# A state-space and MLP block on one core: layer norm in chunks, the middle loop in another order, the fifth scan block in pieces under the output stage

## Chip, cores and metric

One core of a Trainium2 chip. The metric is device time in microseconds (us) of the whole kernel; medians of several runs are quoted. TensorE is called PE, its weight loads PEld, VectorE DVE, ScalarE ACT, the engine that issues transfers SP. Matmuls write into a memory of their own, PSUM. The granted clock is the share of PE's full speed that the profile shows. One execution of the kernel before was slower (485.2 us, mean granted clock 0.82). A line number such as L450 is a line of the kernel that is being spoken of; the kernel before and the changed one have different numbers for the same work.

## The reference

Two branches work on the layer-normed input `xn` (2048 tokens, 640 channels, bf16) and are added to `x`. Branch A is a complex diagonal recurrence over time, branch B a shifted MLP with a second layer norm.

```python
def A(x, ...):                       # 640 complex states
    Bu = einsum("bld,pd->blp", x, B_bar)
    for t in range(L): h = Lam_bar * h + Bu[:, t]
    return 2 * einsum("blp,dp->bld", hseq, C).real + x * Dskip
def B(x, w1, w2, w3, w4):
    h = gelu(layernorm(x) @ w1)
    # ... four channel groups shifted by +1, -1, +2, -2 tokens ...
    x1 = x + shifted(h) @ w2
    return x1 + gelu(layernorm(x1) @ w3) @ w4      # 640 -> 1536 -> 640
xn = layernorm(x)
return x + A(xn, ...) + B(xn, ...)
```

## The kernel before

The 640 states are five blocks of 128 partitions, the 2048 tokens four groups of 512. Each block is projected (`bur`, `bui`), rotated by tables of sine and cosine so that the complex recurrence becomes two real ones, scanned over all 2048 tokens, and rotated back into `hTr`, `hTi`. Gelu is written as x times sigmoid. Names that the profiles use: `x1n` is the input of the third matmul (w3) after its layer norm, `psh` that matmul's result in PSUM, `sg` its sigmoid, `h3h` the product of the two, `acc` the sum that the w4 matmuls build from it; `xrxi` holds a block's projection (later its scan), `bp` a part of its rotation, `ctab` and `stab` its tables; `psy` is the result of the output matmuls. The parts that matter, cut with `...`:

```python
# head: layer norm over all 2048 tokens at once
with tc.tile_pool(name="lrow", bufs=1) as lrow, ..., tc.tile_pool(name="lnp", bufs=1, PSUM) as lnp:
    ...
    for tg in range(TG):
        ...                                        # s1_ps, s2_ps: sums by ones-matmuls
        nc.scalar.copy(out=S1row[:, cols], in_=s1_ps[:])
        nc.scalar.copy(out=S2row[:, cols], in_=s2_ps[:])
    nc.vector.tensor_scalar_mul(out=mean[:], in0=S1row[:], scalar1=inv_d)
    ...                                            # var, Ln, Exp, c1, second Ln and Exp, all 128x2048 f32
    for j in range(DB): ...                        # xnT = xT*r1b + c1b
    for j in range(DB): ...                        # skip: xT += dskip*xnT
# w1 stage
for tg in range(TG): ...                           # xnn, 25 matmuls, sigmoid, copy, h1T pieces

def a_block(b, btr, bti):
    ...                                            # projections, sine tables, rotation
    nc.vector.tensor_tensor_scan(out=gr, data0=rho_bc, data1=bpr, initial=0.0, ...)   # 2048 columns
    nc.vector.tensor_tensor_scan(out=gi, data0=rho_bc, data1=bpi, initial=0.0, ...)
    ...                                            # rotation back

def phase3_h3_half(x1n, fh):
    for f in range(FH):                            # 6 of 12
        ...                                        # psh: 5 matmuls
        nc.scalar.activation(out=sg3[:], in_=psh[:], func=ACT.Sigmoid, scale=GELU_SIG_A)
        nc.vector.tensor_tensor(out=h3h[:, f, :], in0=sg3[:], in1=psh[:], op=ALU.mult)

run_a(0)
st = phase3_tg_pre(0)                              # w2, layer norm 2 -> x1n
h3a = phase3_h3_half(x1n_cur, 0)
phase3_w4_half(st, h3a, 0)
for r in range(TG):
    run_a(r + 1)                                   # whole block r+1
    h3b = phase3_h3_half(x1n_cur, 1)
    if r + 1 < TG: st_next = phase3_tg_pre(r + 1) ...
    phase3_w4_half(st, h3b, 1)
    if r + 1 < TG:
        ...
        h3a = phase3_h3_half(x1n_cur, 0)
        phase3_w4_half(st, h3a, 0)
# output stage: C transposed and scaled, 200 matmuls into psy, fob = xT + psy, 80 transposes, copies, store
```

## Time and profile before

| | before |
|---|---|
| median of 6 runs (range) | 478.42 us (477.19 to 485.2) |
| span of the profiled run | 483.3 us |
| mean granted PE clock in it | 0.82 |
| busy PE / DVE / ACT | 305.0 / 295.7 / 223.4 us |

The profiled run of the kernel before was the slow one of the six (485.2 us), so that some us of what follows are its state and not the kernel. The next view cuts its span at marks of the program: first sigmoid 78.4, first w2 matmul 118.1, rotation of blocks 1 to 4 at 178.5, 248.2, 317.0 and 387.5, dense output matmuls from 429.4. Columns: start and end, length, busy us (and count of instructions) of PE, PEld, DVE, ACT and GpSimd, granted clock, share of the DMA engines, GB/s.

```profile
0.00:78.40 78.40, 18.09 (x50) 6.00 (x51) 39.17 (x80) 31.69 (x26) 2.49 (x7) 0.74 0.36 90
78.40:118.10 39.70, 34.02 (x131) 13.61 (x130) 26.72 (x55) 29.68 (x52) 0.00 (x0) 0.85 0.08 17
...
248.20:317.00 68.80, 48.43 (x201) 20.51 (x200) 45.60 (x54) 34.00 (x43) 0.00 (x0) 0.84 0.13 34
...
429.40:483.30 53.90, 48.02 (x256) 21.52 (x256) 14.50 (x21) 18.22 (x80) 0.00 (x0) 0.94 0.14 49
```

Compare PE's busy time with the length: in the head PE is busy 18 of 78 us, in a round of the middle 48 of 69, in the last stage 48 of 54. Only the last stage is near a limit of one engine.

### The profile page before, as it was taken

To read this page: it belongs to the slowest core of one execution; us is meant where nothing else is said; L and a number is where in the kernel's file an instruction comes from. 1 tells how busy PE (TensorE), PEld (TensorE's weight loads), DVE (VectorE), ACT (ScalarE), POOL (GpSimd) and SP (SyncE) were. 2 spreads that over 40 slices of the span, in tenths; PEclk is the share of its full clock that TensorE was granted. 3 is DMA by queue.
4 is the path that set the end of the run, shared out by engine and by line. 5 is a ranking of instruction groups with operands and counts; after the bars stand their busy time and mean duration, and the time that the engine had idled before them with its cause. 6 is when DMAs were issued, how large, how long until landed. Compare 5 with 4: busy or idle time off the path is not lost.

```text
span 483.3 us, 3602 instructions
## 1 busy us (share of the span) xinstructions
PE 305.0 (63%) x1260; PEld 125.9 (26%) x1260; DVE 295.7 (61%) x400; ACT 223.4 (46%) x334; POOL 2.5 (1%) x7
## 2 busy tenths in 40 slices
PE   2270007798504996285985558982849980679995
PEld 0020002233201342032432123430314430224442
DVE  0203999953999469958149867079635099762221
ACT  5338404769641963495142694241892230213332
POOL 2000000000000000000000000000000000000000
PEclk9996555989855999596998687997687997889998
DMA  9830010011100111110202010201010200431111
GB/s 179 207 130 1 0 37 31 15 26 22 23 0 1 54 33 34 31 41 0 83 11 57 0 42 1 81 1 41 0 41 4 79 14 0 97 40 54 56 54 56
DMA packets 38753, 20.23 MB, mean 42 GB/s; under 512 B 28624, under 2 KB 38096, under 8 KB 38736
## 3 DMA queue, kind: packets, MB, share of 16 engines
q1 hardware_dynamic: 38736, 20.01, 16.1%
q8 instruction: 10, 0.16, 0.1%
q14 instruction: 7, 0.06, 0.0%
HBM read 11.47 MB, written 2.62 MB: 29 GB/s over the span
## 4 chain that ended last, share of the span: by engine, by line
PE 42%; DVE 36%; ACT 10%; SPq 6%; DMA 4%; issue 2%; ACTq 0%; DVEq 0%
PE acc L469 6%; PE ps L393 6%; PE psh L450 6%; DVE xrxi L374 5%; DVE xrxi L377 4%; PE psy L537 4%; PE bur L337 4%; PE psy L542 4%; PE ps L269 3%; PE bui L343 3%; DVE h3h L456 3%; SPq L93 2%; PE pt L551 1%; DMA li_b<-in_A_Lambda_im_dram 1%; DVE bp L365 1%
## 5 line engine op out<-in xcount | busy, mean ns | idle before, releaser
L450 PE MATMUL psh<-x1n,w_sb 128*128 128x512 bf16 x240 | 65.4, 423 | 52.7 <-DVE x1n L428 46.2
L469 PE MATMUL acc<-h3h,w4f 128*128 128x512 bf16 x240 | 60.2, 399 | 11.9 <-DVE h3h L456 11.9
L455 ACT ACTIVATE sg<-psh 128x512 bf16<-128x512 f32 x48 | 28.4, 597 | 75.4 <-PE psh L450 43.9
L269 PE MATMUL ps<-xnn,w_sb 128*128 128x512 bf16 x100 | 29.3, 451 | 41.4 <-DMA w_sb<-in_B_w_dram 39.0
L393 PE MATMUL ps<-h1T,w_sb 128*128 128x512 bf16 x100 | 29.4, 463 | 35.2 <-DVE h3h L456 34.4
L450 PEld LDWEIGHTS <-w_sb 128*128 128x128 bf16 x240 | 25.1, 105 | 90.7 <-issue 66.3
L456 DVE TENSOR_TENSOR h3h<-sg,psh 128x512 bf16<-128x512 bf16 x48 | 32.4, 683 | 17.8 <-ACT sg L455 17.8
L537 PE MATMUL psy<-hTr,CTr 128*128 128x512 bf16 x100 | 38.2, 394 | 5.8 <-DVE CTr L522 4.1
L542 PE MATMUL psy<-hTi,CTi 128*128 128x512 bf16 x100 | 38.5, 397 | 0.6 <-DVE CTi L526 0.4
L552 ACT COPY rowbuf<-pt 128x128 bf16<-128x128 bf16 x80 | 18.2, 267 | 42.7 <-PE pt L551 16.0
L469 PEld LDWEIGHTS <-w4f 128*128 128x128 bf16 x240 | 24.4, 102 | 43.4 <-issue 14.9
L548 DVE TENSOR_TENSOR fob<-xT,psy 128x512 bf16<-128x512 bf16 x20 | 13.7, 687 | 33.7 <-PE psy L542 33.2
L365 DVE TENSOR_TENSOR bp<-xrxi,ctab 128x2048 bf16<-128x2048 bf16 x5 | 6.1, 1223 | 42.6 <-ACT xrxi L341 42.6
L337 PE MATMUL bur<-xnT,btr 128*128 128x512 bf16 x100 | 26.7, 392 | 3.2 <-DMA btr<-in_A_B_re_dram 3.2
L269 PEld LDWEIGHTS <-w_sb 128*128 128x128 bf16 x100 | 11.2, 112 | 58.8 <-issue 50.8
L343 PE MATMUL bui<-xnT,bti 128*128 128x512 bf16 x100 | 25.8, 391 | 0.0
L393 PEld LDWEIGHTS <-w_sb 128*128 128x128 bf16 x100 | 11.5, 115 | 52.9 <-issue 44.8
L341 ACT CAST xrxi<-bur 128x512 bf16<-128x512 f32 x20 | 11.8, 590 | 28.0 <-PE bur L337 28.0
L357 ACT ACTIVATE stab<-u_r 128x2048 bf16<-128x2048 f32 x5 | 9.6, 1910 | 30.7 <-DVE hTi L383 30.2
L374 DVE TENSOR_TENSOR_SCAN xrxi<-rho_col,bp 128x2048 bf16<-128x2048 f32 x5 | 22.1, 4415 | 0.0
L377 DVE TENSOR_TENSOR_SCAN xrxi<-rho_col,bp 128x2048 bf16<-128x2048 f32 x5 | 22.0, 4397 | 0.0
L178 PE MATMUL s_ps<-xT,ones_bf 128*128 128x512 bf16 x20 | 9.0, 484 | 20.4 <-DMA xT<-in_A_x_dram 11.3
(133 smaller groups left out, 480.9 us busy)
## 6 DMA issues: line engine op xcount, KB each, us to landing
w4f<-in_B_w_dram SPq DMA_DIRECT2D x48, 160.0 KB, 2.2
out_dram<-rowbuf SPq DMA_DIRECT2D x4, 640.0 KB, 3.2
w_sb<-in_B_w_dram SPq DMA_DIRECT2D x1, 1920.0 KB, 8.0
w_sb<-in_B_w_dram SPq DMA_DIRECT2D x2, 800.0 KB, 5.8
btr<-in_A_B_re_dram SPq DMA_TRANSPOSE x25, 2.3
bti<-in_A_B_im_dram SPq DMA_TRANSPOSE x25, 2.3
xT<-in_A_x_dram SPq DMA_TRANSPOSE x5, 5.1
CTr<-in_A_C_re_dram SPq DMA_TRANSPOSE x5, 2.9
```

Source lines behind the costliest of these rows:

```text
L269: nc.tensor.matmul(ps[:], lhsT=w1_sb[:, j, i * P : (i + 1) * P], rhs=xnn[:, j, :], start=(j == 0), stop=(j == DB - 1),)
L337: nc.tensor.matmul(bur[:], lhsT=btr[:, j, :], rhs=xnT[:, j, cols], start=(j == 0), stop=(j == DB - 1),)
L343: nc.tensor.matmul(bui[:], lhsT=bti[:, j, :], rhs=xnT[:, j, cols], start=(j == 0), stop=(j == DB - 1),)
L374: nc.vector.tensor_tensor_scan(out=gr, data0=rho_bc, data1=bpr, initial=0.0, op0=ALU.mult, op1=ALU.add,)
L377: nc.vector.tensor_tensor_scan(out=gi, data0=rho_bc, data1=bpi, initial=0.0, op0=ALU.mult, op1=ALU.add,)
L393: nc.tensor.matmul(ps[:], lhsT=w2_sb[:, j, i * P : (i + 1) * P], rhs=h1T[:, j, 2 + tg * 512 : 2 + tg * 512 + 512], start=(j == 0), stop=(j ...
L450: nc.tensor.matmul(psh[:], lhsT=w3_sb[:, j, ff * P : (ff + 1) * P], rhs=x1n[:, j, :], start=(j == 0), stop=(j == DB - 1),)
L455: nc.scalar.activation(out=sg3[:], in_=psh[:], func=ACT.Sigmoid, scale=GELU_SIG_A)
L456: nc.vector.tensor_tensor(out=h3h[:, f, :], in0=sg3[:], in1=psh[:], op=ALU.mult)
L469: nc.tensor.matmul(accs[i][:], lhsT=w4fs[ff][:, i * P : (i + 1) * P], rhs=h3h[:, f, :], start=False, stop=(ff == FB - 1),)
L537: nc.tensor.matmul(psy[:], lhsT=CTr[:, b, i * P : (i + 1) * P], rhs=hTr[:, b, cols], start=(k == 0), stop=False,)
L542: nc.tensor.matmul(psy[:], lhsT=CTi[:, b, i * P : (i + 1) * P], rhs=hTi[:, b, cols], start=False, stop=(b == NPB - 1),)
```

## The change

Its intent is to stop the engines from taking turns. Five things are changed:

1. The first layer norm runs in four chunks of 512 tokens, straight from PSUM; its Ln and Exp share one table, loaded early.
2. The memory is laid out anew: the layer norm no longer takes over the memory of the parameter tiles, its PSUM sums have two buffers each, and the projection of block 0 goes into the w1 stage. The skip products come after the w1 work of their group.
3. `h3x`: ScalarE copies `psh` to bf16, so that VectorE's product reads no PSUM.
4. The middle loop pairs block r with token group r and spreads the parts of the block between the halves of the MLP.
5. The fifth block is scanned in four pieces inside the output stage.

```diff
-        for j in range(DB): ...                     # full-width layer norm, then all of skip
+        for tg in range(TG):
+            r2b, last_exp = ln1_tg(tg)              # 512 columns, load_ln_exp(...) early
+            r2bs.append(r2b)
+        for tg in range(TG):
+            with tc.issue_after(last_exp.ins):
+                ph2_tg(tg, r2bs[tg])                # w1 stage
+                a_bu_tg(bt0, tg)                    # projection of block 0
+            skip_tg(tg)
 ...
                 nc.scalar.activation(out=sg3[:], in_=psh[:], func=ACT.Sigmoid, scale=GELU_SIG_A)
-                nc.vector.tensor_tensor(out=h3h[:, f, :], in0=sg3[:], in1=psh[:], op=ALU.mult)
+                h3x = bsq.tile([P, 512], BF16, name="h3x")
+                nc.scalar.copy(out=h3x[:], in_=psh[:])
+                nc.vector.tensor_tensor(out=h3h[:, f, :], in0=sg3[:], in1=h3x[:], op=ALU.mult)
 ...
+        st_cur = b1_pre(0)
+        a_tables(0)
         for r in range(TG):
-            run_a(r + 1) ...
+            h3a = b2_h3_half(st_cur, 0)
+            a_fwd(b)                                # b = r; rotation
+            b3_w4_half(st_cur, h3a, 0, accs)
+            a_scans(b)
+            if r + 1 < TG: st_next = b1_pre(r + 1)
+            h3b = b2_h3_half(st_cur, 1)
+            a_back(b)
+            if b + 1 < NPB:
+                a1(b + 1)                           # projection of the next block
+                a_tables(b + 1)
+            b3_w4_half(st_cur, h3b, 1, accs)
 ...
         for tg in range(TG):
+            a_last(NPB - 1, [tg])                   # fifth block, 512 columns
             ...                                     # output matmuls of tg
```

## The prediction

> **What bounds the kernel now.** I read the busy table first, to see whether one engine is near its limit.
>
> ```profile
> PE 305.0 (63%) x1260; PEld 125.9 (26%) x1260; DVE 295.7 (61%) x400; ACT 223.4 (46%) x334; POOL 2.5 (1%) x7
> ```
>
> None is. TensorE and VectorE are busy 63% and 61%; together that is 601 us in a span of 483, so for at least three quarters of the span not both are working: they largely take turns. The waits of the whole span say who hands the turn to whom (microseconds in total, times, longest):
>
> ```profile
> PE psh L450 <- DVE x1n L428: 46.2, 4, 24.5
> DVE bp L365 <- ACT xrxi L341: 42.6, 4, 13.9
> PE ps L269 <- DMA w_sb<-in_B_w_dram: 39.0, 1, 39.0
> PE ps L393 <- DVE h3h L456: 34.4, 3, 11.5
> ```
>
> Three of these are one loop: PE waits for VectorE's normalised rows (L428), then VectorE waits until PE and ScalarE have delivered the next block's projection (L341), then PE waits for the h3h products that stand in VectorE's queue behind the scans (L456). The fourth is the head: PE has nothing to do until the layer norm over all 2048 tokens and its weights are there. Next the chain that ended last, one round of the middle (start, length, what):
>
> ```profile
> 248.18 1.23 DVE bp L365
> ...
> 256.87 4.33 DVE xrxi L374
> 261.21 4.32 DVE xrxi L377
> ...
> 271.83 7.15 PE ps L393 x25
> ...
> 288.02 1.28 ACT L417
> 291.04 0.76 DVE x1n L427 x2
> 292.19 5.00 PE psh L450 x15
> 297.19 1.13 PE acc L463 x5
> 298.32 3.37 PE psh L450 x15
> 301.69 6.74 PE acc L469 x30
> 308.43 1.13 PE bur L337 x5
> ...
> 316.96 1.22 DVE bp L365
> ```
>
> The chain alternates: VectorE 24.6 us (rotate, two scans, rotate back), PE and ScalarE 19.4 us (L393, statistics, tables of sine, Ln, Exp) up to x1n, then PE 25 us (psh 9.5, acc 6.7, the projections 8.5). The round is 316.96 - 248.18 = 68.8 us. The stretches of that size confirm that no engine fills it (stretch, length, then busy by engine):
>
> ```profile
> 239.70:308.40 68.70, 48.33 (x201) 20.47 (x200) 45.59 (x53) 34.00 (x43) 0.00 (x0) 0.84 0.13 34
> ```
>
> PE 48 and DVE 46 of 68.7 (an overlap-free sum would be 94): there are some 20 us of alternation to win per round, and a floor near 48.
>
> **What the Trainium skill says.** "TensorE: Matmul & The Clock Gate", Part 1 (the HAM clock gate): a PE idle for about 3.4 us falls to half rate and needs about as long to recover. The trace agrees: after the 7.4 us idle at 292.19 fifteen matmuls take 5.0 us, a later fifteen 3.4 us. Each long idle so costs 1.5 us beyond itself. "ScalarE: Activation LUTs", What ACT_TABLE_LOAD costs: 1283 ns and a drain of about 1380 ns. Here the load is 1.28 us and the next activation starts 0.02 us later (288.02+1.28, Exp at 289.32), so I take 1.3 per switch. "VectorE: DVE Perf Modes", Mode 1× and Mode 2×_1P: operands in PSUM run at the base rate, packed bf16 in SBUF at twice that. The trace agrees: h3h, with one PSUM operand, averages 683 ns, x1n from bf16 in SBUF 416 ns; back to back 0.60 and 0.34.
>
> **The change part by part.** I followed the compiled order of each engine in the changed kernel and put on it the start-to-start times of this trace (matmul of 512 columns 0.225, bf16 pass over 2048 columns 1.14, over 512 0.34, sigmoid plus copy pair 0.97, table load 1.3).
>
> *Head.* The layer norm goes from one pass over 2048 tokens to four of 512. Before, a chain of full-width f32 passes runs from 35.8 (mean) to 68 and the first sigmoid starts at 78.4. After, the VectorE parameter arithmetic, now with 4.6 us of table argument among it, ends near 29; then mean, and chunks 0 and 1 give xnT by 29+1+4+5.2+5.2 = 45. ScalarE has the tables of block 0 (four passes of 1.9) and about nine table loads in the same queue and sits at the end: its last Exp at 61, one load, first sigmoid at **62.5**. VectorE has chunks 2 and 3 done then as well (63). Gain 16.
>
> *w1 stage with the projections of block 0.* Per 512 tokens VectorE has xnn 5 x 0.34, nine h1T pieces 3.3, skip 5 x 0.55: 7.7; PE has 35 matmuls, 7.9; ScalarE 5 pairs and 2 copies, 5.9. Four groups plus 4.6 us of table argument, less what ran already: 33 us, to **96**. Before, this point (first L393) was 118. Gain 22 so far; the DMA wait is inside it.
>
> *First round.* Block 0's rotation starts at 96.5. In VectorE's queue stand rotation 6.8, x1 3.0, statistics 1.8, scan 4.3, x1n and x 5.1, scan 4.3, h3h 2.0, rotation back 6.8: 34.5. The rest of the round as below, 30: next rotation at **161**; before, block 1's was at 178.5. Gain 17.5 so far. (The old order started block 1's rotation before block 0's tokens had finished their second h3 half; the new one doesn't, so 4.5 us of the 22 are given back.)
>
> *Steady rounds.* Between x1n and the projections the old chain had psh half, identity and acc half: 308.43-292.19 = 16.2, and x1n 2.3 before it (289.98 to 292.19). The new order puts the half-0 matmuls after the projections, where they run under the next block's rotation and first scan (11 us of VectorE work against 15 matmul groups, 30 acc later); only half 1 remains in between, at the pace of ScalarE: six sigmoid-and-copy pairs, 5.8. So 68.8 - 16.2 - 2.3 + 5.8 = 56.1. The h3x copy is 12 x 0.48 = 5.8 us more ScalarE and 12 x 0.26 = 3.1 us less VectorE per round; only half 1 of it is on the path and is in the 5.8. Walking the queues for the other hops gives 54; I use **55.5**, twice: 216.5, 272. Before these were 69.7 and 68.8 (248.2, 317). Gain 27.
>
> *Fifth block.* Its rotation and scans leave the middle and go, in four pieces, under the output matmuls, where VectorE was busy 17.8 of 57.3 us. So one round vanishes: before, block 4's rotation started at 387.5 and dense output matmuls at 429.4. After, block 3's at 272: rotation, scans and back with half-0 matmuls 22-24, half-1 pairs behind a table load to 31, projections with sine passes between the copies to 43, acc to 47, C transposes (ten at 1.27 us, once the w3 buffer is free) to 46 and their VectorE scaling to 48.5, first piece of the fifth block (12 x 0.34 + 2 x 1.1) to 54, with 24 of 200 output matmuls (5.4 us) done meanwhile. Then 429.4 to 483.3 = 54 less 5.4: 272 + 54 + 48.6 = 374.6. From block 3's rotation to the end it was 483.3 - 317 = 166.3 and becomes 102.6: gain 64, on top of the 45 already won at that point.
>
> Sum: 96.5 + 64.5 + 111 + 102.6 = **375** of span. The profiled run was a slow one (485.2 against the median 478.4), which would take 4 off; run times exceed the span by 2; hand-offs between engines that I left out (0.1 to 0.2 us each, some 30 on the path) add about 5. Prediction **378**.
>
> **Rivals.** (a) *ScalarE becomes the link.* h3x copies, sigmoid, squares, sine passes, Ln and Exp share one in-order queue, with five table loads per round. For: in the compiled order the squares of x1 stand between sine passes, and a sigmoid pair with its own table load between them and Ln. Its sum is about 37 us per round, so it isn't a throughput bound, but it can delay x1n or the projections. 60 to 62 per round: 392. (b) *VectorE is the bound.* About 41 us per round in an in-order queue; h3h products stand before x1n in it, as they stood behind the scans before. If each such place costs 2 us: 385 to 390. Against: the cheaper h3h and the lost PSUM read. (c) *Less alternation than I think, and full-rate PE.* With 45 us of matmuls per round and no 11 us idles, PE stays warm; 50 per round and a head at 55: 358. (d) *The head gives nothing*, because many short passes pay their fixed cost and the loads of Ln/Exp repeat: 16 us lost, 392. (e) *No gain at all* would need the rounds to stay at 69; even then the removed fifth round saves over 30 us.
>
> **Range and chances.** Errors of 3 us per round in four rounds, 8 in the head and 5 in the end, partly independent, give about -18/+24: 360 to 402. All rivals are faster than before by over 10%, so 0.97 for faster; what is left is for a stall that I did not see in the order.
>
> **What would show it.** Rotation starts in the changed profile at about 96, 161, 216 and 272; the first sigmoid near 62; the wait of psh for x1n falls from 46 to under 15 us in total, that of L393 for h3h from 34 to under 8; h3h products near 416 ns; the full-width scans number four pairs; output matmuls dense for the last 50 us. VectorE's busy sum drops to about 280, ScalarE's rises to about 248 (48 h3x copies of 0.59). I am wrong if rounds exceed 62 (then see who ends the projections' wait), if the first sigmoid comes after 72, or if output matmuls wait for the fifth block's pieces.

## The result

| | before | after |
|---|---|---|
| median (range, runs) | 478.49 us (476.9 to 485.2, 16) | 377.74 us (375.85 to 379.41, 8) |
| span of the profiled run | 483.3 us (slow) | 376.9 us (fast) |
| busy PE / DVE / ACT | 305.0 / 295.7 / 223.4 us | 291.4 / 286.8 / 239.5 us |

The ratio is 0.789 (95% interval 0.7875 to 0.7909). A ratio here is the mean time of one kernel's runs over that of the other's of the same rounds, so it isn't quite the ratio of the medians quoted. Executions over 1.5% slower than the fastest of the same kernel are left out of the means. The time is 100.7 us less by the medians, and the prediction of 378.0 holds.

The busy table of the changed kernel:

```profile
PE 291.4 (77%) x1260; PEld 122.4 (32%) x1260; DVE 286.8 (76%) x509; ACT 239.5 (64%) x401; POOL 2.5 (1%) x7
```

The same number of matmuls, and nearly the same VectorE work, in a span shorter by a fifth: the time came from waits and not from work. Here are the waits of the whole span that answer to the four shown before:

```profile
ACT sg L482 <- DVE h3h L485: 24.0, 11, 3.6
...
PE psh L477 <- ACT h3x L484: 14.5, 9, 2.8
...
PE psh L477 <- DVE x1n L462: 8.7, 1, 8.7
DVE bp L263 <- ACT xrxi L228: 8.4, 3, 3.6
...
PE acc L500 <- DVE h3h L485: 2.7, 1, 2.7
```

`psh` waits for `x1n` 8.7 us instead of 46.2, and once instead of four times; the rotation waits for the projections 8.4 us instead of 42.6; the 34.4 us of w2 matmuls behind `h3h` are gone. What is new is short and frequent: `psh` and the sigmoid wait for a buffer (14.5 and 24.0 us). Now the stretches, cut at the same marks, with the rotation of blocks 0 to 3 at 96.8, 160.0, 212.9 and 266.8:

```profile
0.00:62.00 62.00, 23.82 (x55) 7.02 (x56) 40.12 (x123) 42.89 (x56) 2.49 (x7) 0.76 0.38 80
62.00:96.50 34.50, 29.68 (x126) 12.59 (x126) 33.48 (x86) 24.20 (x47) 0.00 (x0) 0.94 0.19 65
96.50:160.00 63.50, 49.77 (x215) 20.97 (x214) 51.82 (x76) 44.52 (x61) 0.00 (x0) 0.92 0.13 36
160.00:212.90 52.90, 45.84 (x197) 19.57 (x195) 42.12 (x52) 37.73 (x54) 0.00 (x0) 0.94 0.15 41
212.90:266.80 53.90, 47.15 (x212) 20.43 (x210) 41.67 (x52) 38.98 (x55) 0.00 (x0) 1.00 0.18 49
266.80:319.00 52.20, 45.39 (x200) 19.68 (x199) 45.72 (x63) 32.95 (x50) 0.00 (x0) 0.97 0.29 64
319.00:376.90 57.90, 49.78 (x263) 22.13 (x262) 31.84 (x60) 18.22 (x80) 0.00 (x0) 0.94 0.13 46
```

Against the table before: the head gives 16.4 us (78.4 to 62.0), the w1 stage 5.2, the first round takes 3.1 back (60.4 to 63.5), the two steady rounds give 16.8 and 14.9, the stretch from the last full rotation to dense output matmuls 60.2 (317.0 to 429.4 was 112.4; now 52.2), and the last stage takes 4.0 back. Together 106.4, which is 483.3 - 376.9; some 6 of them are the slow state of the profile before.

A steady round now is still a chain, here as the chain that ended last gives it (start, length, what):

```profile
160.02 1.23 DVE bp L263
...
172.28 4.33 DVE xrxi L275
...
182.51 1.92 ACT stab L250
...
197.55 2.29 PE psh L477 x5
...
204.71 1.08 PE bur L224 x5
...
212.92 1.23 DVE bp L263
```

VectorE carries it for 22.5 us (rotation, scans, rotation back), ScalarE for 15 (sine passes, squares, table loads), PE for 15, of which 7.2 are MLP matmuls and the rest projections. The prediction had 24.6, 19.4 and 25 us for these three parts of the old round: PE's part has shrunk most, by 10 us, the middle part by 4. The next round divides otherwise: in it ScalarE carries the chain from 235.4 to 255.8 us.

### The profile page after: what moved, and what is told of

It is laid out like the page before. It is cut to its first block, busy times and chain, and to the rows that moved or that the text cites. A ratio compares the mean times of both kernels' runs of the same rounds, so it can differ in the third digit from the quotient of the medians.

```text
span 376.9 us, 3776 instructions
## 1 busy us (share of the span) xinstructions
PE 291.4 (77%) x1260; PEld 122.4 (32%) x1260; DVE 286.8 (76%) x509; ACT 239.5 (64%) x401; POOL 2.5 (1%) x7
## 4 chain that ended last, share of the span: by engine, by line
DVE 43%; ACT 21%; PE 20%; SPq 8%; issue 5%; DMA 2%; ACTq 0%; DVEq 0%
DVE xrxi L275 5%; PE psy L579 4%; PE psy L575 4%; PE psh L477 3%; PE bur L224 3%; DVE h1T L395 3%; SPq L112 3%; DVE xrxi L300 2%; DVE xrxi L272 2%; PE bui L230 2%; ACT u_r L251 2%; ACT L482 2%; PE acc L500 2%; DVE h3h L485 2%; ACT sqb L439 2%
## 5 line engine op out<-in xcount | busy, mean ns | idle before, releaser
L477 PE MATMUL psh<-x1n,w_sb 128*128 128x512 bf16 x240 | 59.5, 394 | 24.2 <-ACT h3x L484 14.5
L477 PEld LDWEIGHTS <-w_sb 128*128 128x128 bf16 x240 | 24.0, 100 | 60.3 <-issue 36.4
L385 PE MATMUL ps<-xnn,w_sb 128*128 128x512 bf16 x100 | 25.6, 417 | 15.1 <-ACT xb L392 12.0
L484 ACT CAST h3x<-psh 128x512 bf16<-128x512 f32 x48 | 29.2, 608 | 0.0
L485 DVE TENSOR_TENSOR h3h<-sg,h3x 128x512 bf16<-128x512 bf16 x48 | 19.3, 416 | 10.7 <-ACT h3x L484 10.6
L429 PE MATMUL ps<-h1T,w_sb 128*128 128x512 bf16 x100 | 22.6, 378 | 0.6 <-DVE x L434 0.5
L385 PEld LDWEIGHTS <-w_sb 128*128 128x128 bf16 x100 | 10.5, 105 | 30.4 <-issue 20.9
L329 ACT ACTIVATE sq<-xT 128x512 bf16<-128x512 bf16 x20 | 11.7, 621 | 11.6 <-DMA xT<-in_A_x_dram 10.8
L390 ACT ACTIVATE sg<-ps 128x512 bf16<-128x512 f32 x20 | 12.0, 602 | 9.8 <-DVE h1T L395 6.5
L506 ACT CAST xT<-acc 128x512 bf16<-128x512 f32 x20 | 10.2, 606 | 12.7 <-PE acc L500 12.7
L272 DVE TENSOR_TENSOR_SCAN xrxi<-rho_col,bp 128x2048 bf16<-128x2048 f32 x4 | 17.7, 4422 | 0.1
L275 DVE TENSOR_TENSOR_SCAN xrxi<-rho_col,bp 128x2048 bf16<-128x2048 f32 x4 | 17.7, 4416 | 0.0
```

The costliest lines, as they stand in the source:

```text
L385: nc.tensor.matmul(ps[:], lhsT=w1_sb[:, j, i * P : (i + 1) * P], rhs=xnn[:, j, :], start=(j == 0), stop=(j == DB - 1),)
L477: nc.tensor.matmul(psh[:], lhsT=w3_sb[:, j, ff * P : (ff + 1) * P], rhs=x1n[:, j, :], start=(j == 0), stop=(j == DB - 1),)
L484: nc.scalar.copy(out=h3x[:], in_=psh[:])
L485: nc.vector.tensor_tensor(out=h3h[:, f, :], in0=sg3[:], in1=h3x[:], op=ALU.mult)
```

## Experiments

Twelve kernels ran, on three chips, each timed against the kernel before on its own chip, and all gave the right result; the profiled run of each of the twelve was fast. The kernel before was at 478.08, 478.57 and 479.06 us there, so that about 1 us of a difference between medians can be the chip. The first four start from the changed kernel and undo one part each.

### u_order: the old order of the middle

```diff
-        st_cur = b1_pre(0)
+        a_fwd(0); a_scans(0); a_back(0)
+        st_cur = b1_pre(0); accs = get_accs()
+        h3a = b2_h3_half(st_cur, 0); b3_w4_half(st_cur, h3a, 0, accs)
         for r in range(TG):
+            b = r + 1
+            a1(b); a_tables(b)
+            if b < NPB - 1: a_fwd(b); a_scans(b); a_back(b)
+            h3b = b2_h3_half(st_cur, 1)
             ...                    # pre of r+1, acc half 1, then h3 and acc half 0 of r+1
```

> The changed kernel with the old order of the middle: block b+1 projected, rotated and scanned before the second h3 half of the tokens of round b, next half 0 and its acc in one go before the projections. Head, h3x copy and piecewise last block stay. My theory is that the order is worth 69 - 53 = 16 us in each of the full rounds: with two to three such rounds 410 to 425. The rival, that the copy h3x and its early release of PSUM made the rounds shorter and not the order, says 378 to 390.

Measured: 437.39 us, ratio 0.914 (0.911 to 0.916), 60 us above the changed kernel and more than either expectation. Rounds are 64.9 us (rotations at 160.1, 225.0, 289.8) against 53.4, and the stretch from the rotation of block 3 to the end is 145.4 us against 110.1. The waits of u_order, whole span:

```profile
ACT stab L250 <- DVE hTi L283: 40.4, 4, 11.8
DVE bp L263 <- ACT xrxi L228: 34.9, 4, 12.4
...
PE psh L477 <- DVE x1n L462: 30.0, 4, 8.7
...
PE acc L500 <- DVE h3h L485: 28.7, 3, 9.6
```

The three waits of the old loop (the last three lines) are back with most of their size, about once per round, in a kernel that keeps everything else of the change; the third now stands before `acc` and not before the w2 matmuls. So the order makes the difference, in two shares: about 11.5 us in each of the two steady rounds, and 35 us at the end, where the old pairing (block r+1 beside token group r) leaves more of the MLP for after the last whole block: 543 matmuls and transposes follow the rotation of block 3, in the changed kernel 463 (200 + 263).

### u_tail: the fifth block whole, before the output stage

```diff
+            if b + 1 == NPB - 1:
+                a_fwd(b + 1); a_scans(b + 1); a_back(b + 1)
 ...
-            a_last(NPB - 1, [tg])
```

> The changed kernel with the fifth block rotated, scanned and rotated back over all 2048 tokens before the output stage, not in four pieces under it. Theory: the first output matmul of block 4 then waits for about 22 us of VectorE work instead of 6, of which the C scaling hides nothing since it stands in the same queue: 390 to 395. The rival: TensorE works on blocks 0 to 3 meanwhile and only PSUM buffers bound it, and the pieces slow the output stage (57.9 us after, 53.9 before): 376 to 384.

Measured: 392.21 us, ratio 0.8205 (0.818 to 0.823): 14.5 us above, as expected. One wait of its profile is the whole answer, PE before the output matmuls that need block 4:

```profile
PE psy L578 <- DVE hTr L282: 14.0, 1, 14.0
```

### u_h3x: without ScalarE's copy

```diff
-                h3x = bsq.tile([P, 512], BF16, name="h3x")
-                nc.scalar.copy(out=h3x[:], in_=psh[:])
-                nc.vector.tensor_tensor(out=h3h[:, f, :], in0=sg3[:], in1=h3x[:], op=ALU.mult)
+                nc.vector.tensor_tensor(out=h3h[:, f, :], in0=sg3[:], in1=psh[:], op=ALU.mult)
```

> The changed kernel without the ScalarE copy h3x: VectorE multiplies the sigmoid by the PSUM tile, as before the change. Theory of the prediction: on the path the copies cost 6 x 0.48 = 2.9 us per round on ScalarE between Exp and the projections, VectorE gains 3.1 us per round; the two nearly cancel: 374 to 382. The rival: a PSUM tile is then freed by VectorE's queue, behind scans of 4.3 us, so TensorE stalls in half 0 and the rounds grow by 5 or more: 390 to 400.

Measured: 386.73 us, ratio 0.808 (0.806 to 0.810), 9.0 us above, between the two expectations. The prediction had treated the copy as neutral or a small cost. Its rounds take 67.0, 54.8 and 54.7 us against 63.2, 52.9 and 53.9, so that the first round loses most. The wait in u_h3x shows why:

```profile
PE psh L477 <- DVE h3h L483: 25.3, 15, 3.2
```

With the copy, a PSUM buffer is free as soon as ScalarE has read it. Without it, the buffer is free only after the product, which stands in VectorE's queue behind scans of 4.4 us. The early release is one part of the copy's gain, the faster product (416 instead of 680 ns, 48 times) another; the run doesn't part them, but the wait is there in 25.3 us, and the changed kernel has 14.5 us for ScalarE's copy in its place.

### u_head: full-width layer norm in the changed kernel

```diff
-        for tg in range(TG):
-            r2b, last_exp = ln1_tg(tg)          # four chunks of 512
+        r2b, last_exp = ln1_full()              # the old passes over 2048 columns
```

> The changed kernel with the first layer norm again in full-width passes over 2048 tokens (w1 keeps its own buffer, so its load is still early, and Exp still writes bf16). If the chunking of the norm is what gave the head its gain, as the prediction reckons (first sigmoid at 62 instead of 78), the first sigmoid comes 12 to 16 us later and the time is about 390. The rival: the gain of the head comes from what else changed there (the w1 load no longer waits for a buffer, no f32-to-bf16 casts, the block-0 tables in the gaps): then within 4 us of the changed kernel, 374 to 382.

Measured: 381.98 us, ratio 0.798 (0.794 to 0.802), 4.2 us above. The first sigmoid is at 66.6 us against 61.9; the sigmoids of the w1 stage in the changed kernel, and then in u_head (minimum, median and maximum ns, first and last start):

```profile
L390 ACT ACTIVATE sg<-ps x20: 597/597/643, 61.9 to 95.2; 128x512 bf16<-128x512 f32 x20
```

```profile
L392 ACT ACTIVATE sg<-ps x20: 597/597/617, 66.6 to 99.6; 128x512 bf16<-128x512 f32 x20
```

Of the 16.4 us that the head gained, undoing the chunks gives back less than 5, and my theory, which put all of it there, falls. In this kernel the mean over all tokens starts at 27.9 us, in the kernel before at 35.8: something ahead of the mean had been late. From the mean to the first `xnn` both take nearly the same time (34.5 and 34.8 us). Then the matmuls of the kernel before wait 3.3 us more, from 71.0 to 74.3, for the load of w1: it starts only at 69.6, when the layer norm gives its memory up, and lands at 74.2. In u_head and in the changed kernel w1 has memory of its own and has landed by 37.6. No run takes that away alone.

### b_apar: the kernel before with one wait taken away

In the kernel before, the copies of the sums (`S1row`) start at 25.0 us, just as the last parameter operation is done: the layer norm's rows lie in the memory of the parameter tiles, and its PSUM sums have one buffer. This run keeps the parameter tiles in memory of their own.

```diff
-    with tc.tile_pool(name="apar", bufs=1) as apar:
+    apar = ctx.enter_context(tc.tile_pool(name="apar", bufs=1))   # opened ahead of coefp, kept to the end
 ...
-        tc.tile_pool(name="lnp", bufs=1, space=bass.MemoryType.PSUM) as lnp,
+        tc.tile_pool(name="lnp", bufs=2, space=bass.MemoryType.PSUM) as lnp,
```

> The kernel before, in which the layer norm's row buffers no longer take over the memory of the parameter tiles and its two PSUM sums have two buffers each; nothing else. In the kernel before, the copies of the sums waited for the last parameter operation until 25.0 us. If the head's other delays (the part that full-width layer norm in the changed kernel did not bring back) come from this wait: about 8 us earlier mean, total 468 to 472. If the later part of the head (inputs' loads, skip ahead of the first normalised tile) hides it: 476 to 479.

Measured: 468.70 us, ratio 0.9785 (0.9735 to 0.983), 9.9 us below the kernel before (the interval is clear of no change, but reaches across a gain of 2%). The copies of the sums in the kernel before, and then in b_apar (minimum, median and maximum ns, first and last start):

```profile
L186 ACT COPY S1row<-s_ps x4: 585/585/585, 25.0 to 35.2; 128x512 f32<-128x512 f32 x4
```

```profile
L187 ACT COPY S1row<-s_ps x4: 567/580/598, 17.3 to 23.9; 128x512 f32<-128x512 f32 x4
```

The mean moves from 35.8 to 25.6 us, by 10.2, and the first sigmoid from 78.4 to 68.1. The delay passes through to the end whole. It is a wait for memory: it is not in the data flow and is gone when the tile pools no longer overlap. The two edits of this run (parameter memory, PSUM buffers) were not told apart; the first copy comes 7.7 us earlier and the last 11.3, since they also follow each other faster.

### u_skip: the skip products ahead of the w1 work

```diff
+        for tg in range(TG):
+            skip_tg(tg)
         for tg in range(TG):
             with tc.issue_after(last_exp.ins):
                 ph2_tg(tg, r2bs[tg])
                 a_bu_tg(bt0, tg)
-            skip_tg(tg)
```

> In the changed kernel, the skip products of all token groups go into VectorE's queue ahead of the first normalised tile for w1, as in the kernel before. Twenty pairs of about 0.25 and 0.34 us are 12 us in one piece, of which ScalarE's last Exp at 60 us hides what fits before it. If VectorE is the one that is late at the head: first sigmoid at 66 or later, 382 to 386. If ScalarE's queue sets the first sigmoid: 377 to 380.

Measured: 387.79 us, ratio 0.811 (0.808 to 0.814), 10 us above, somewhat more than the 4 to 8 expected. ScalarE has its table by 61.7 us, then waits for PE, which waits for `xnn` (start, length, idle before):

```profile
72.21 0.60 ACT L390 ACTIVATE sg<-ps 128x512 bf16<-128x512 f32 x1 [10.52 <-PE ps L385]
```

VectorE has skip products in its queue from 61.9 to 69.4 us, behind those of earlier groups, and only then `xnn`. So in the changed kernel where the skip stands is worth more than the chunking.

### i_tail: the pieces of the fifth block one group ahead

The last stage was predicted 48.6 us long and is 57.9. This run asked whether the pieces are the reason.

```diff
+        a_last(NPB - 1, [0])
         for tg in range(TG):
-            a_last(NPB - 1, [tg])
 ...
                 nc.vector.tensor_tensor(out=ob[:], in0=xT[:, i, cols], in1=psy[:], op=ALU.add)
+                if i == 0 and tg + 1 < TG: a_last(NPB - 1, [tg + 1])
```

> In the changed kernel, with the pieces of the fifth block one token group ahead: piece tg+1 goes into VectorE's queue right after the first output sum of token group tg. Theory: the last stage was predicted 9 us too short because output matmuls wait behind pieces; yet by the stretches only about 2.3 us of idle PE lie between 319 and 350 us, so 375 to 377. Rival: the pieces hold up the whole stage and are the full 9 us: 368 to 370.

Measured: 378.99 us, ratio 0.792 (0.790 to 0.794); the interval overlaps that of the changed kernel, and both expectations were for less. It tells less than I had hoped: the scans of pieces 2 to 4 start at 323.7, 331.6 and 339.7 us, in the changed kernel at 324.6, 331.7 and 339.7, so the scheduler had already put them ahead, and the edit hardly moved anything. What stands is the count of idle PE: from 319 to 371 us it is 52.0 - 49.1 = 2.9 us, not 9.

### i_inpl, i_lnexp and i_tables: the waits that were left

i_inpl goes at the 24.0 and 14.5 us of waits for buffers: the sigmoid is written into `h3h` itself and `h3x` gets five buffers.

```diff
-                nc.scalar.activation(out=sg3[:], in_=psh[:], func=ACT.Sigmoid, scale=GELU_SIG_A)
-                h3x = bsq.tile([P, 512], BF16, name="h3x")
+                nc.scalar.activation(out=h3h[:, f, :], in_=psh[:], func=ACT.Sigmoid, scale=GELU_SIG_A)
+                h3x = bsg.tile([P, 512], BF16, name="h3x")          # bsg: bufs=5
```

> The sigmoid is written straight into the product's tile, so that its two small buffers go and the copy of the matmul's result gets five buffers instead of two. The changed kernel still shows 14.5 us of matmuls that wait on the copies and 24.0 us of ScalarE that waits for products to free the buffers. If these waits still bound a round: rounds of about 51 instead of 52.9 to 53.9, total 366 to 373. If they only hide behind the VectorE order of a round (VectorE busy 45 of 53 us, with the rotation and scans in one piece): 375 to 380, and the waits move to another name.

Measured: 378.68 us, ratio 0.791 (0.7865 to 0.795): no difference. The sigmoid's wait for products is no longer among the large ones, the rotation of block 3 comes 3 us earlier (263.8), and the end stays where it was; instead ScalarE's sine pass waits 23.1 us for VectorE's rotation back (5.3 before). The buffers were not the bound.

i_lnexp takes one table load off the chain of the second layer norm:

```diff
-            nc.scalar.activation(out=var3[:], in_=mean3[:], func=ACT.Square)
+            load_ln_exp(nc.scalar.activation(out=var3[:], in_=mean3[:], func=ACT.Square))
```

> The second layer norm of each token group gets the same early load of the one table that holds both functions as the head has. It takes one table load of 1.28 us off the chain from mean to normalised tile in four groups. If that chain still bounded a round: up to 4 x 1.3 = 5 us less, 372 to 375. If it no longer does (wait of the matmuls for the normalised tile is only 8.7 us in all): 377 to 379.

Measured: 382.65 us, ratio 0.799 (0.796 to 0.803), slower by about 5, which neither expectation had. Rotations stay within 1.3 us of the changed kernel's, and block 3's comes 0.4 us later (267.2), so that the chain gained nothing; the order of the last round changed, and 2.9 of the 3.3 us between the two profiled runs are lost from there on. The first C transpose of the output stage starts when PE has gone past the last `psh` matmul, to the projection behind it. The first transposes in the timeline of the changed kernel, and then of i_lnexp (start, length):

```profile
296.07 1.13 SPq L553 DMA_TRANSPOSE CTr<-in_A_C_re_dram  x1
```

```profile
301.39 1.13 SPq L553 DMA_TRANSPOSE CTr<-in_A_C_re_dram  x1
```

They start 5.3 us later, because PE in i_lnexp does all 30 matmuls of `acc` half 0 ahead of the last `psh` half (294.7 to 301.4 us). The first output matmul follows by as much (318.3, changed kernel 312.9).

i_tables makes the tables of the next block early, in a second pair of buffers, paid for with one `x1` buffer and the sigmoid in place:

```diff
+    ctabs = [...2 tiles...]; stabs = [...2 tiles...]     # used by b % 2
-        tc.tile_pool(name="bx1", bufs=2) as bx1,
+        tc.tile_pool(name="bx1", bufs=1) as bx1,
 ...
             a_fwd(b)
+            if b + 1 < NPB: a_tables(b + 1)
 ...
-                a_tables(b + 1)
```

> Two sets of sine tables, so that the tables of the next block are made right after the rotation of this one, away from the layer norm of the next token group; paid for with one x1 buffer instead of two. ScalarE's table passes (about 9 us in one piece per round) then stand beside the bu copies. If the in-order ScalarE queue bounds a round: rounds of 48 to 50, total 358 to 368. If PE with its pitch (45 to 47 us busy of 53) and VectorE bound it: 374 to 380. The single x1 buffer may cost up to 3 us per round, then over 380.

Measured: 393.46 us, ratio 0.821 (0.816 to 0.826), 16 us slower. Already the first rotation is late (103.1 us, changed kernel 96.8), and three rounds take 182.0 us against 170.0. ScalarE's squares now wait for `x1` (22.3 us between 160 and 285). The freed place in the chain and the lost buffer are mixed in this run, so it doesn't show what the second tables alone would do.

### i_bu0 and i_best: block 0's projection in the head

```diff
             r2bs.append(r2b)
+            if tg > 0: a_bu_tg(bt0, tg - 1)
+        a_bu_tg(bt0, TG - 1)
 ...
-                a_bu_tg(bt0, tg)
```

> In the changed kernel, the 40 matmuls of block 0's projection and their 8 copies go into the head, after each token group's layer norm, in place of the w1 stage. PE has nothing else to do there; the w1 stage loses 8.6 us of PE and 4.8 us of ScalarE. If PE bounds the w1 stage (30 of 34.5 us): first w2 matmul 5 to 8 us earlier, 370 to 373. If the copies stand in ScalarE's queue between the Ln and Exp passes, which set the first sigmoid: the 4.8 us come back in the head, 376 to 381.

Measured: 380.83 us, ratio 0.796 (0.793 to 0.798), about 3 slower. The first sigmoid moves from 61.9 to 69.3 us, since eight copies and a table load more stand in ScalarE's queue; the w1 stage is shorter, and the first w2 matmul is at 91.5 (96.4), the rotation of block 0 at 88.8 (96.8). Then all is given back: the rotation goes into VectorE's queue ahead of the last `h1T` pieces and of the x1 sums, and `x1n` starts at 113.9 us, in the changed kernel at 112.9. PE waits for it longer (8.7 in the changed kernel):

```profile
PE psh L479 <- DVE x1n L464: 11.7, 1, 11.7
```

i_best is i_bu0 with the edits of i_inpl and i_tail.

> The three together: projection of block 0 in the head, the sigmoid in place with five copy buffers, the pieces of the fifth block one group ahead. If their gains add: 366 to 371. If each only moves the wait to another queue: 375 to 380.

Measured: 381.83 us, ratio 0.798 (0.795 to 0.801). That is above both expectations: nothing adds up, and no run is faster than the changed kernel.

## Why the prediction was right

**The total** is right (378.0 predicted, 377.74), but with errors that cancel, and that they do so this closely is luck. By its own milestones, predicted and then measured: rotation of block 0 at 96.5 and 96.8; the first round 64.5 and 63.2 us; two rounds 111.0 and 106.8; from block 3's rotation to dense output 54 and 52.2; the rest 48.6 and 57.9. The differences are +0.3, -1.3, -4.2, -1.8 and +9.3, together +2.3, and 374.6 + 2.3 = 376.9, the span. The prediction's step from 375 to 378 (4 off for the slow state, 2 and 5 added) is an estimate that no run tests. VectorE's busy time fell to 286.8 us and not 280, ScalarE's rose to 239.5 and not 248.

**Slips in the working.** "For at least three quarters of the span not both are working" is turned around: 600.7 - 483.3 = 117 us is the least time for which both work, so it is at most three quarters. The queue of the first round adds up to 34.1 and not 34.5, and from 289.98 to 292.19 is 2.2 and not 2.3. None of them moves the total by more than half a us.

**The head**: the milestone (62.5, measured 61.9) is right and the cause is named wrong. The prediction put the gain down to chunking. The runs give chunking 4 to 5 us, the release of the parameter memory (with PSUM buffers) about 10 in the kernel before, and the skip's place about 10 in the order of the changed kernel; they overlap. The 39.0 us wait of the head, named for w1's DMA, was in the prediction rightly left inside the layer norm's gain: only its last 3.3 us are the load's own. In b_apar the same matmuls wait 41.6 us and the list of waits names VectorE, but their first starts at 64.03 us, 0.14 after w1 has landed (63.89), just as in the kernel before (74.32 after 74.19): it is the same load, named otherwise.

**The first round and the steady rounds**: shown right in mechanism by u_order, where the waits come back. The rounds are 2 us shorter than predicted. The trace before was slow, with 0.225 us from matmul to matmul; in the fast run of the changed kernel five take 1.08 us, so 0.216. The rounds of the kernel before that took 69.7 and 68.8 us there take 67.9 and 68.1 in the fast run of b_apar, so about 1.2 of the 2 us can be the state; the rest wasn't settled. It also puts a size on the order: from 68.0 to u_order's 64.9 us a round is what else changed, and from 64.9 to 53.4 is the order, 11.5 us and not the 16 expected. PE's granted clock goes with it, 0.87 in these rounds of u_order, 0.94 and 1.00 in the changed kernel; its share of the 11.5 us was not told apart.

**The copy `h3x`**: the step that counted "only half 1 of it" as a cost on the path missed its use. It takes 608 ns a time on ScalarE, as foreseen. But without it the kernel is 9 us slower, and its `psh` matmuls wait 25.3 us for VectorE's products.

**The last stage** is the mis-sized term: "Then 429.4 to 483.3 = 54 less 5.4". The 24 output matmuls that are to be done early were subtracted, but the stretch before had lost them as well: in the kernel before, the 11.4 us ahead of 429.4 hold 25 of its matmuls. That stretch of the kernel before (its last stage is in the table of stretches above), and then the last stage of the changed kernel up to its last transposes:

```profile
418.00:429.40 11.40, 6.72 (x25) 1.79 (x25) 9.43 (x17) 0.00 (x0) 0.00 (x0) 0.95 0.60 95
```

```profile
319.00:371.00 52.00, 49.11 (x259) 21.86 (x258) 31.62 (x60) 17.35 (x76) 0.00 (x0) 0.97 0.11 39
```

The 5.4 us were counted twice. The other 4 of the 9.3 are seven more matmuls than before (263 and 256, about 1.5 us at 0.216: only 17 of the 24 were done early) and some 2.6 us more of idle PE (2.9 of 52.0; in the kernel before 0.3 of the 47.6 from 429.4 to 477). The waits from 319 us on say where PE stood still:

```profile
PE pt L587 <- DVE fob L584: 3.0, 4, 0.8
...
PE psy L575 <- DVE hTr L306: 2.2, 1, 2.2
```

The transposes `pt` wait for output sums, which share VectorE's queue with the pieces; that the pieces delay them is likely and not shown. The second line is the prediction's own sign of being wrong, output matmuls that wait for the fifth block's pieces: it came about once, for 2.2 us until 318.97, which is in the stretch before.

**The rivals.** Neither ScalarE as the link (392) nor VectorE as the bound (385 to 390) came about at that size; part of the first is true: 15 us of one round's chain, and 20 of the next, are ScalarE's. Rival (c), less alternation, was the nearest of them in the rounds: 53.4 us lies between its 50 and the 55.5 of the prediction. Rivals (d) and (e), a head or rounds without gain, did not come about.

**Do the parts add?** Undoing the order (59.7), the tail (14.5), `h3x` (9.0), the chunks (4.2) and the skip's place (10.1), and the 9.9 of the memory in the kernel before, make 107.4 us, where the change gives 100.7. The parts overlap by some 7 us. w1's own memory, the early load for Ln and Exp and the place of block 0's projection were not undone by a run of their own (i_bu0 only moves the last).

## What to carry to other kernels

When several engines are each busy 60% and hand over to each other, move whole phases of work until each engine's queue has something to do that doesn't need the others; here undoing the order alone costs 60 of the 100 us. Look in the start of a kernel for waits that are not in the data flow, such as a tile that takes over memory of another, since b_apar got 10 us for two small edits. A list of waits names the releaser that came last by the profile, so check a large one against the landing of the loads, as for w1. And when a stage of the old profile is used as a yardstick for the new one, count what it holds (matmuls from mark to mark) before subtracting anything from it; afterwards, expect that shortening a wait off the path, as in i_inpl, gives nothing.

## What the Trainium skill lacked or had wrong

- "ScalarE: Activation LUTs", What ACT_TABLE_LOAD costs, gives 1283 ns and a drain of about 1380 ns for a switch. In every run here each load takes 1283 ns, and wherever the next activation does not wait for data (25 of 31 times in the changed kernel) it starts within 0.02 us; no drain was seen.
- The same page, Table sets, says that Ln followed by Exp needs one load, since one set holds both. As built, the middle of the changed kernel loads twice for them in each of its four groups (ahead of L452 and of L454), in three of them with no function of another set between; in the fourth a sigmoid stands there. With the explicit early load, i_lnexp has only two loads fewer in all (29, from 31), since in two later rounds a sigmoid comes between, and it is 5 us slower: the count of loads was not the bound.
- "TensorE: Matmul & The Clock Gate", Part 2, gives 215.7 ns from matmul to matmul of 512 columns. The fast runs agree (0.216). The slow state of a program on one core, with 0.225 us and a mean clock of 0.82 in the profile before (0.84 to 0.86 in its fast runs), is on none of the pages that I read.
- No page that I read gives a case in which an extra copy of a PSUM tile by ScalarE pays by releasing the buffer early; there is only the general advice to empty PSUM promptly. Here the kernel without the copy is 9.0 us slower (u_h3x), with VectorE's scans ahead of the products.
